# An attention-and-experts kernel whose build-time scheduler is switched to its detailed timing model

## The chip, the cores and the metric

The kernel runs on 1 core of one Trainium2 chip. The metric is the device time of one execution in microseconds (us); lower is better. The inputs come from a fixed seed.

## The reference, cut to what matters

Four batches of 10048 rows of width 128 pass through an attention with 49 agents, and the resulting 40192 rows through a mixture of 16 experts (4 groups of 4), of which each row takes one.

```python
def _attn_ref(q, k, v, agents):
    def sm(a, b):                      # softmax of scale * a b^T
        ...
    a2k = sm(agents, k)
    agent_v = a2k @ v
    q2a = sm(q, agents)
    return (q2a @ agent_v)
def _moe_ref(x, w_group, w_expert, w1, w2):
    ...                                # best group, then best expert of that group
            h = np.maximum(xg[mask_e] @ w1[g, e], 0.0)
            ye = h @ w2[g, e]
            out[tok_idx] = combined[:, None] * ye
```

## The kernel before

**Stages.** The work goes through the batches in the order `SEQ = (1, 2, 3, 0)`. An opening (to about 54 us) does keys, values and agents of the first batch and chooses the expert that most of its rows take. Then come three batches of *own tiles*: 20 tiles of 512 rows each, and each tile is sent through the batch's main expert in 8 *units*, 480 units in all. The last batch is *sorted*: its rows are scattered by expert into `sorted_rows` and read back in order, 164 units more, from about 720 us on.

**A unit** (functions `first`, `evicted`, `second`) is: on TensorE (PE) two matmuls of 512 columns into a PSUM bank `ph`, from the turned weights `et` of the tile and the expert's `wbuf`; on ScalarE (ACT) `hh<-ph`, the relu in 16 bits; on VectorE (DVE) `hl<-ph,hh`, what the 16 bits left over; then on PE three matmuls into `po`, two from `hh` and one from `hl`. `ph` has three banks (pool `ps1`), so the `ph` pair of a unit has to wait for the `hl` of the third unit before. In the source `second` runs `LAG = 8` units behind `first`.

```python
LAG = 8
            pending.append(first(x, k))
            for _ in range(2):
                if len(pending) > LAG:
                    run_second()
            advance(at + (k + 1) * each)
```

**Side work.** Beside the units of one batch runs the attention of the next. `advance` steps *lanes* (generators) after each unit and gives out so much ACT and DVE work per unit (`RATE`, 900 and 1100 ns); a lane that yields `HOP` rests for 2 units, so that what the next step reads is there. The names in it: `xf` are loaded keys or queries, `xh` (ACT) and `xl` (GpSimd, POOL) their 16-bit halves, and PE's `at<-agh,xl` the scores; `S` holds the scores of the keys, 10 tiles to a chunk, 8 chunks. `key_max` sends the maxima through PE (`at<-dg,ones`) and back to `mb` on DVE. `value_less` then subtracts it on DVE (`S<-S,mb`), `value_exp` takes the exponent on ACT (`S<-S,shift`), `value_split` makes `sh` and `vh` (ACT), `vl` (DVE) and `sl` (POOL), and `value_products` are PE's `at<-sh,vh`. The source steps these stages chunk by chunk (`skewed`). `mq`, `ef` and `rows` are the same for queries, `es` and the turned `et` come from them; `oo<-po,oo` on DVE ends a tile, with factors that were loaded from `cwt`.

**What sets the order.** The source gives each engine a program order; on leaving the `TileContext` at line 1847 a scheduler goes through all instructions and writes the order in which each engine gets them, which is fixed from then on. Each engine works its list off strictly in order: an instruction that waits holds up all behind it. Nearly all instructions are recorded by one helper and so stand at line 140.

## Time and profile before

| | |
|---|---|
| median of 3 runs | 914.24 us (911.54 to 914.42) |
| the profiled execution, its own time | 907.38 us |
| its span | 905.1 us |
| PE busy | 844.7 us, 93% |
| DVE busy | 710.8 us, 79% |
| ACT busy | 613.8 us, 68% |
| POOL busy | 462.9 us, 51% |
| mean granted TensorE clock | 0.982 of full speed |

Busy is the time in which an engine worked at any instruction; PE's matmuls overlap, so their single durations are longer than the distance at which they follow each other. The difference of 2.3 us between time and span lies ahead of the first and behind the last instruction. The profiled execution is 6.9 us shorter than the median of the three runs.

### The profile page before, as it was taken

Reading aid. Unit: us, or ns where it says so; the run is one execution under the profiler, and the core shown is the slowest. Engines: PE = TensorE matmul, PEld = TensorE weight load, DVE = VectorE, ACT = ScalarE, POOL = GpSimd, SP = SyncE. Lnnn points to the kernel's source line nnn. Section 1 sums busy time; section 2 is a strip of 40 time slices with the busy share of each in tenths; the row PEclk is TensorE's granted clock in tenths of the full one; section 3 lists DMA queues with packets and bytes.
Section 4 is the critical chain, followed back from the end, with each engine's and each line's share of the span. In section 5 each row is a group of like instructions: output and inputs, shape, how many; then the busy total and the mean of one; then the engine's idle time right before and its main releaser. Section 6 shows DMA issues by size and latency. Waiting matters only on the chain.

```text
span 905.1 us, 22546 instructions
## 1 busy us (share of the span) xinstructions
PE 844.7 (93%) x8668; PEld 502.2 (55%) x8669; DVE 710.8 (79%) x1442; ACT 613.8 (68%) x1078; POOL 462.9 (51%) x616
## 2 busy tenths in 40 slices
PE   4889999999797999898999999999999999999995
PEld 3745455555354555454455555554444477777775
DVE  7767898886799886688989689799977666766663
ACT  6568897867486777677678787766565555555552
POOL 4387495446426451838474343646555214444454
PEclk9989999999899999999999999999999999999998
DMA  9677436453554564434536222334756445555542
GB/s 360 245 244 272 139 108 225 157 163 128 173 170 130 169 196 147 156 115 152 169 112 242 83 75 104 112 102 151 230 176 212 138 140 165 174 190 187 176 141 98
DMA packets 58578, 149.95 MB, mean 166 GB/s; under 512 B 8702, under 2 KB 19830, under 8 KB 58460
## 3 DMA queue, kind: packets, MB, share of 16 engines
q1 hardware_dynamic: 53307, 138.11, 45.4%
q0 software_dynamic: 5152, 10.30, 3.2%
q8 instruction: 70, 1.15, 0.5%
q14 instruction: 49, 0.39, 0.1%
HBM read 108.33 MB, written 38.71 MB: 162 GB/s over the span
## 4 chain that ended last, share of the span: by engine, by line
PE 41%; DVE 8%; ACT 3%; DMA 2%; issue 2%; POOL 2%; POOLq 0%; ACTq 0%; DVEq 0%
PE po L140 24%; PE ph L140 12%; PE at L140 6%; DVE hl L140 3%; POOL xl L304 1%; ACT hh L140 1%; DMA out<-oo,er 1%; DVE vl L140 1%; DMA vf<-v 1%; DVE mq L140 1%; DVE ef L140 1%; ACT vh L140 1%; DVE oo L140 0%; POOL out L1485 0%; ACT es L140 0%
## 5 line engine op out<-in xcount | busy, mean ns | idle before, releaser
L140 DVE SCALAR_TENSOR_TENSOR hl<-ph,hh 128x512 f16<-128x512 f32 (+1 forms) x562 | 374.6, 677 | 125.7 <-ACT hh L140 122.0
L140 ACT ACTIVATE hh<-ph 128x512 f16<-128x512 f32 (+1 forms) x562 | 330.0, 594 | 188.2 <-PE ph L140 110.5
L140 PEld LDWEIGHTS <-wbuf 128*128 128x128 f16 (+2 forms) x2812 | 241.2, 97 | 282.6 <-issue 50.3
L140 PE MATMUL ph<-et,wbuf 98*128 98x512 f16 (+2 forms) x1048 | 317.4, 378 | 17.7 <-DVE hl L140 17.1
L140 PE MATMUL po<-hh,wbuf 128*128 128x512 f16 (+1 forms) x960 | 287.2, 379 | 0.0
L304 POOL TENSOR_TENSOR xl<-xf,xh 128x256 f16<-128x256 f32 x278 | 183.2, 696 | 137.1 <-ACT xh L140 124.4
L140 PE MATMUL po<-hl,wbuf 128*128 128x512 f16 (+1 forms) x480 | 181.3, 378 | 0.0
L1485 POOL DMA_INDIRECT out<-oo,er x82 | 80.7, 984 | 110.7 <-ACT hh L140 53.0
L140 PE MATMUL po<-wbuf,hh 128*128 128x128 f16 x1312 | 116.6, 219 | 0.0
L1199 POOL DMA_INDIRECT sorted_rows<-rows,slot x79 | 79.0, 1000 | 67.7 <-ACT hh L140 47.1
L140 PE MATMUL po<-wbuf,hl 128*128 128x128 f16 x656 | 112.9, 219 | 0.0
L140 PEld LDWEIGHTS <-hh 128*128 128x128 f16 x1312 | 99.2, 98 | 9.0 <-issue 9.0
L140 ACT ACTIVATE xh<-xf 128x1280 f16<-128x1280 f32 (+2 forms) x58 | 72.5, 1255 | 17.2 <-PE at L140 12.2
L510 POOL TENSOR_TENSOR sl<-S,sh 128x245 f16<-128x245 f32 (+2 forms) x51 | 37.8, 764 | 53.5 <-ACT sh L140 53.5
L140 PEld LDWEIGHTS <-hl 128*128 128x128 f16 x656 | 64.2, 98 | 0.0
L847 POOL TENSOR_TENSOR rows<-ef,rows 128x245 f16<-128x245 f32 (+1 forms) x62 | 39.9, 666 | 42.8 <-ACT rows L140 42.8
L140 PEld LDWEIGHTS <-xh 128*128 128x128 f16 x1166 | 46.3, 98 | 21.6 <-issue 2.2
L140 DVE SCALAR_TENSOR_TENSOR hl<-at,hh 128x512 f16<-128x512 f32 x82 | 55.8, 680 | 0.0
L140 DVE SCALAR_TENSOR_TENSOR vl<-vf,vh 128x640 f16<-128x640 f32 (+2 forms) x51 | 48.4, 956 | 7.2 <-ACT vh L140 7.2
L140 ACT ACTIVATE et<-at 98x512 f16<-98x512 f16 (+3 forms) x81 | 47.4, 596 | 8.8 <-PE at L140 8.7
L140 ACT ACTIVATE hh<-at 128x512 f16<-128x512 f32 x82 | 49.5, 604 | 0.0
L140 DVE TENSOR_TENSOR oo<-po,oo 128x512 f32<-128x512 f32 (+1 forms) x60 | 40.3, 672 | 9.6 <-PE po L140 6.2
(330 smaller groups left out, 1042.8 us busy)
## 6 DMA issues: line engine op xcount, KB each, us to landing
wbuf<-wdr SPq DMA_DIRECT2D x22, 832.0 KB
vf<-v SPq DMA_DIRECT2D x28, 645.0 KB
xf<-qT SPq DMA_DIRECT2D x27, 640.0 KB
xf<-kT SPq DMA_DIRECT2D x25, 640.0 KB
cols<-oo SPq DMA_DIRECT2D x60, 256.0 KB
oo<-cwt SPq DMA_DIRECT2D x57, 256.0 KB
erow<-rows SPq DMA_DIRECT2D x12, 490.0 KB
er<-sorted_rows SPq DMA_DIRECT2D x19, 256.0 KB
```

The costliest lines, as they stand in the source:

```text
L140: ins = f(*a, **k)
L304: pool.tensor_sub(out=xl[:, a:z], in0=xf[:, a:z], in1=xh[:, a:z])
L510: pool.tensor_sub(out=sl[0:m, y][:, z], in0=x[:, z], in1=sh[0:m, y][:, z])
L847: pool.tensor_sub(out=x0[:, a:z, NA:2 * NA], in0=ef[:, a:z], in1=x0[:, a:z, 0:NA])
L1199: ins = pool.indirect_dma_start(out=sorted_rows[:, :], out_offset=bass.IndirectOffsetOnAxis(ap=at, axis=0), in_=x, in_offset=None, bounds_ ...
L1485: ins = pool.indirect_dma_start(out=out, out_offset=bass.IndirectOffsetOnAxis(ap=to, axis=0), in_=y, in_offset=None, bounds_check=N - 1, o ...
```

## The change

The `TileContext` is told to schedule with its detailed timing model. No line of the computation is touched, no instruction is added or taken away: the same 8,552 matmuls, 1,441 DVE, 1,076 ACT and 611 POOL instructions and 422 loads and stores of the SP queue are put into another order.

```diff
-    with tile.TileContext(nc) as tc, ExitStack() as ctx:
+    with tile.TileContext(nc, schedule_with_timeline_sim=True) as tc, ExitStack() as ctx:
         build(ctx, tc, *args, out, cols)
```

What moves: of PE's matmuls of the opening and the own tiles hardly one keeps its place (by as much as 169 places), on DVE the places change by up to 58, on ACT by up to 32, on POOL by up to 20. In the sorted tiles, from about 720 us on, the order of all engines is the same as before but for a few neighbours. In the opening ACT takes the exponent `ef` of the first queries behind one `xh` more, and on SP one store to `sorted_rows` goes ahead of three loads. Three places show the pattern. In the names the number is that of the tile, so that the same name is the same buffer in both orders.

**DVE, the first batch's own units 33 to 45**, where the scores `S_834` of the next batch lose their maximum `mb_1827`. Before:

```order
L140 COPY mb_1827<-at_1800 128x49
L140 TENSOR_TENSOR S_834<-S_834,mb_1827 128x490
L140 SCALAR_TENSOR_TENSOR hl_1819<-ph_1815,hh_1818 128x512
L140 TENSOR_TENSOR oo_1718<-po_1720,oo_1718 128x512
L140 TENSOR_TENSOR S_834<-S_834,mb_1827 128x490
L140 SCALAR_TENSOR_TENSOR hl_1840<-ph_1836,hh_1839 128x512
L140 TENSOR_TENSOR S_834<-S_834,mb_1827 128x490
L140 SCALAR_TENSOR_TENSOR hl_1858<-ph_1854,hh_1857 128x512
L140 SCALAR_TENSOR_TENSOR vl_1852<-vf_1829,vh_1851 128x640
L140 SCALAR_TENSOR_TENSOR hl_1872<-ph_1868,hh_1871 128x512
L140 SCALAR_TENSOR_TENSOR hl_1884<-ph_1880,hh_1883 128x512
```

With the change:

```order
L140 COPY mb_1827<-at_1800 128x49
L140 SCALAR_TENSOR_TENSOR hl_1742<-ph_1738,hh_1741 128x512
L140 TENSOR_TENSOR S_834<-S_834,mb_1827 128x490 x3
L140 TENSOR_REDUCE mq_1956<-at_1774 128x10
L140 TENSOR_TENSOR S_834<-S_834,mb_1827 128x490 x4
L140 TENSOR_TENSOR S_834<-S_834,mb_1827 128x392
L140 TENSOR_TENSOR S_834<-S_834,mb_1827 64x49
L140 SCALAR_TENSOR_TENSOR hl_1753<-ph_1749,hh_1752 128x512
L140 SCALAR_TENSOR_TENSOR hl_1768<-ph_1764,hh_1767 128x512
```

The nine subtractions, which stood one or two between two `hl` over some 14 units, now stand in a row, with `mq` among them, ahead of `hl_1753`, the `hl` of unit 36. The same happens to the nine of the third batch (all nine between two `hl`) and of the fourth (eight of them and an `oo`).

**ACT, the same stretch**, where the exponents of these chunks are taken. Before:

```order
L140 ACTIVATE hh_1839<-ph_1836 128x512
L140 ACTIVATE S_834<-S_834,shift_122 128x490
L140 ACTIVATE vh_1851<-vf_1829 128x1280
L140 ACTIVATE hh_1857<-ph_1854 128x512
L140 ACTIVATE S_834<-S_834,shift_122 128x490
L140 ACTIVATE sh_1849<-S_834 128x490
L140 ACTIVATE hh_1871<-ph_1868 128x512
L140 ACTIVATE hh_1883<-ph_1880 128x512
L140 ACTIVATE S_834<-S_834,shift_122 128x490
L140 ACTIVATE hh_1913<-ph_1910 128x512
```

With the change:

```order
L140 ACTIVATE hh_1767<-ph_1764 128x512
L140 ACTIVATE S_834<-S_834,shift_122 128x490 x2
L140 ACTIVATE et_1925<-at_1920 98x512
L140 ACTIVATE sh_1849<-S_834 128x490
L140 ACTIVATE S_834<-S_834,shift_122 128x490
L140 ACTIVATE et_1932<-at_1927 98x512
L140 ACTIVATE sh_1988<-S_834 128x490
L140 ACTIVATE hh_1793<-ph_1790 128x512
L140 ACTIVATE S_834<-S_834,shift_122 128x490
L140 ACTIVATE et_1949<-at_1944 98x512
L140 ACTIVATE S_834<-S_834,shift_122 128x490 x3
L140 ACTIVATE S_834<-S_834,shift_122 128x392
L140 ACTIVATE S_834<-S_834,shift_122 64x49
```

Where one or two instructions stood between two `hh` in these rows, seven now stand between `hh_1767` and `hh_1793` and seven between `hh_1793` and `hh_1808` (the last row is followed by `hh_1808`).

**PE, unit 41 and the next**, the matmuls of `first` (into `ph`) and of `second` (from `hh` and `hl`). Before:

```order
L140 MATMUL ph_1836<-et_1677,wbuf0_90 128x512
L140 LDWEIGHTS wbuf0_90
L140 MATMUL ph_1836<-et_1677,wbuf0_90 128x512
L140 LDWEIGHTS wbuf0_90
L140 MATMUL po_1845<-hh_1714,wbuf0_90 128x512
L140 LDWEIGHTS wbuf0_90
L140 MATMUL po_1845<-hh_1714,wbuf0_90 128x512
L140 LDWEIGHTS wbuf0_90
L140 MATMUL po_1845<-hl_1715,wbuf0_90 128x512
L140 LDWEIGHTS wbuf0_90
L140 MATMUL ph_1854<-et_1677,wbuf0_90 128x512
```

With the change:

```order
L140 MATMUL ph_1836<-et_1677,wbuf0_90 128x512
L140 LDWEIGHTS wbuf0_90
L140 MATMUL ph_1836<-et_1677,wbuf0_90 128x512
L140 LDWEIGHTS wbuf0_90
L140 MATMUL po_1845<-hl_1794,wbuf0_90 128x512
L140 LDWEIGHTS wbuf0_90
L140 MATMUL po_1845<-hh_1808,wbuf0_90 128x512
L140 LDWEIGHTS wbuf0_90
L140 MATMUL po_1845<-hh_1808,wbuf0_90 128x512
L140 LDWEIGHTS wbuf0_90
L140 MATMUL ph_1854<-et_1677,wbuf0_90 128x512
```

Before, a `ph` pair is followed by the `po` matmuls of the unit eight earlier (`hh_1714` belongs to unit 33, `ph_1836` to unit 41). Now it is followed by the `hl` matmul of unit 38 (`hl_1794`) and the `hh` matmuls of unit 39 (`hh_1808`). In 406 of 449 units counted the `hl` matmul stands exactly three `ph` pairs behind its own, where it was eight.

## Rows read from the trace of the kernel before

**Rows 1.** The page: engines' busy time, share of span, instructions.
```profile
PE 844.7 (93%) x8668; PEld 502.2 (55%) x8669; DVE 710.8 (79%) x1442; ACT 613.8 (68%) x1078; POOL 462.9 (51%) x616
```

**Rows 2.** Busy time by stretch: start:end, length, PE, PEld, DVE, ACT, POOL, clock, DMA, GB/s.
```profile
0.00:75.00 75.00, 54.30 (x732) 39.22 (x734) 55.08 (x148) 49.33 (x77) 42.40 (x63) 0.93 0.78 288
75.00:640.00 565.00, 534.38 (x5094) 289.26 (x5092) 475.56 (x982) 420.90 (x733) 300.72 (x433) 0.98 0.44 147
600.00:720.00 120.00, 120.00 (x630) 56.16 (x629) 100.85 (x255) 73.03 (x127) 60.99 (x61) 1.00 0.54 177
720.00:890.00 170.00, 169.99 (x2338) 131.09 (x2336) 115.15 (x188) 94.22 (x185) 72.78 (x74) 1.00 0.50 167
```

**Rows 3.** Whom PE waited for from 75 to 640 us: total, times, longest.
```profile
PE ph L140 <- DVE hl L140: 16.7, 12, 5.6
PE at L140 <- POOL xl L304: 6.3, 7, 2.8
PE at L140 <- DVE vl L140: 1.5, 3, 0.6
PE at L140 <- ACT et L140: 1.4, 1, 1.4
PE at L140 <- DVE ef L140: 1.4, 2, 0.9
PE at L140 <- DVE cwo L140: 1.0, 2, 0.6
PE at L140 <- ACT es L140: 0.9, 2, 0.5
PE at L140 <- DVE dd L140: 0.7, 1, 0.7
```

**Rows 4.** Timeline of PE, units without side work: start, us, what.
```profile
104.94 0.60 PE L140 MATMUL ph<-et,wbuf 98*128 98x512 f16 x2
105.37 0.60 PE L140 MATMUL po<-hh,wbuf 128*128 128x512 f16 x2
105.80 0.38 PE L140 MATMUL po<-hl,wbuf 128*128 128x512 f16 x1
106.02 0.60 PE L140 MATMUL ph<-et,wbuf 98*128 98x512 f16 x2
```

**Rows 5.** Timeline of ACT and DVE, the same stretch.
```profile
105.57 0.60 ACT L140 ACTIVATE hh<-ph 128x512 f16<-128x512 f32 x1 [0.48 <-PE ph L140]
106.19 0.68 DVE L140 SCALAR_TENSOR_TENSOR hl<-ph,hh 128x512 f16<-128x512 f32 x1
...
108.81 0.66 DVE L140 TENSOR_TENSOR S<-S,mb 128x490 f32<-128x490 f32 x1
109.38 0.68 DVE L140 SCALAR_TENSOR_TENSOR hl<-ph,hh 128x512 f16<-128x512 f32 x1
...
109.97 0.69 ACT L140 ACTIVATE S<-S,shift 128x490 f32<-128x490 f32 x1
110.57 0.60 ACT L140 ACTIVATE sh<-S 128x490 f16<-128x490 f32 x1
111.07 1.07 ACT L140 ACTIVATE hh<-ph 128x512 f16<-128x512 f32 x2
```

**Rows 6.** Timeline of DVE, instructions that met POOL at work.
```profile
224.15 7.22 DVE L140 TENSOR_TENSOR coe<-coe,cog 128x16 f32<-128x16 f32 x1
284.91 3.57 DVE L140 SCALAR_TENSOR_TENSOR vl<-vf,vh 128x640 f16<-128x640 f32 x1
411.23 1.05 DVE L140 TENSOR_TENSOR S<-S,mb 128x490 f32<-128x490 f32 x1
```

**Rows 7.** Timeline of POOL and PE around two long waits.
```profile
218.73 12.61 POOL L304 TENSOR_TENSOR xl<-xf,xh 128x256 f16<-128x256 f32 x20
...
430.48 0.59 PE L140 MATMUL ph<-et,wbuf 98*128 98x512 f16 x2 [3.24 <-DVE hl L140]
```

**Rows 8.** Groups by form: count, busy us, mean ns, idle before.
```profile
L140 DVE TENSOR_TENSOR S<-S,mb 128x490 f32<-128x490 f32 x28 | 21.5, 792 | 0.1
L140 DVE TENSOR_REDUCE mq<-at 128x10 f32<-128x490 f32 x26 | 17.0, 656 | 3.5 <-PE at L140 3.4
L140 ACT ACTIVATE S<-S,shift 128x490 f32<-128x490 f32 x21 | 15.2, 723 | 1.0 <-DVE S L140 0.9
L140 ACT ACTIVATE xh<-xf 128x1280 f16<-128x1280 f32 x51 | 64.7, 1272 | 16.1 <-PE at L140 11.4 <-POOL xl L304 2.4 <-DVE vl L140 1.0
L304 POOL TENSOR_TENSOR xl<-xf,xh 128x256 f16<-128x256 f32 x271 | 181.0, 704 | 137.1 <-ACT xh L140 124.4 <-PE at L140 9.8 <-DMA vf<-v 2.5
```

**Rows 9.** Busy time and clock in the stretches of two waits, each with what followed.
```profile
226.40:231.40 5.00, 0.06 (x3) 0.00 (x0) 5.00 (x2) 1.27 (x1) 4.94 (x8) 0.95 0.16 52
231.40:237.40 6.00, 5.37 (x27) 2.31 (x27) 5.81 (x21) 1.76 (x4) 0.00 (x0) 0.50 0.34 89
380.70:384.50 3.80, 0.99 (x18) 0.50 (x15) 1.56 (x3) 1.45 (x2) 3.80 (x8) 1.00 0.70 229
384.60:387.80 3.20, 3.20 (x23) 1.55 (x22) 1.92 (x4) 2.24 (x5) 3.20 (x6) 0.50 0.69 210
```

## The prediction

> **What bounds the kernel now.** I read the engines' shares first: PE works in 93% of the span, the next engine in 79% [rows 1]. Then the stretches: from 600 us on PE never rests, and in the sorted tiles (720 to 890 us) it is busy all the time at full clock [rows 2]. So time can be won or lost in two places only: the opening, with some 21 us of PE idle in 75 us, and the own tiles from 75 to 640 us, where PE is busy for 534.4 of 565 us, which leaves 30.6 us idle [rows 2]. Whom PE waited for there [rows 3] gives 16.7 us to DVE's `hl`, 6.3 us to POOL's `xl` and 6.9 us to six smaller groups. The waits for `hl` are the third-unit rule: no bank, no next `ph`. The largest of them was no matter of order: one small DVE multiplication took 7.22 us [rows 6] while POOL went through 20 `xl` without a pause [rows 7]; another, 3.24 us, stands in [rows 7].
>
> The **slack of the bank loop** decides what an order may do. Without side work a unit takes PE 106.02 - 104.94 = 1.08 us, in it 0.43 us for `ph`, 0.43 for `po` from `hh`, 0.22 for `po` from `hl` [rows 4]. From the start of `ph` at 104.94 us to the end of its `hl` at 106.19 + 0.68 us [rows 5] it is 1.93 us. The bank is wanted after three units, 3.25 us. So ACT or DVE may fall behind by 1.3 us before PE stands; PE's own side work in those units makes it about 2.0 us at most places.
>
> **The change, part by part.** No work is added, so only idle time and clock can move.
>
> *Side work in rows on DVE and ACT: a loss.* At the first place of the printed order nine `S<-S,mb` and one `mq` stand between the `hl` of units 35 and 36. On DVE such a subtraction takes 0.57 us up to the next start (108.81 to 109.38 us) [rows 5], `mq` about the same less overlap [rows 8]. Seven full subtractions, a shorter one, the small one and `mq` make about 5.3 us, and `hl` ends 0.68 us later: 6.0 us behind the last `hl`. That one ends 1.93 us after the `ph` of unit 35 began, and the `ph` of unit 36 begins 0.93 us after it, by PE's matmuls in between; so the bank of unit 36 is free 1.0 + 6.0 = 7.0 us after its `ph` began. PE, by its own printed order with the prices of [rows 4], has 4.4 us of work until the `ph` of unit 39 asks for it. It stands for 2.6 us there. On ACT, exponents follow each other at 0.60 us (109.97 to 110.57 us) and others at 0.50 [rows 5]: seven between two `hh` are 3.7 to 4.1 us against 1.08 to 2.1 us of PE.
>
> I did the same addition for all units from the 12th to the 480th: what DVE (and ACT) has between two `hl` (two `hh`), at the mean of its form less the overlap, minus what PE has between the two `ph`; the excess is carried on, and what goes beyond the slack is PE's wait. The order before has at most 2.7 us of DVE work in one unit, none over 3.25; the new one has 12 units over 3.25 us on each of the two engines, up to 6.5. The sum over all units:
>
> - slack 1.3 us: 5.8 us before, 47.5 us now
> - slack 1.6 us: 3.8 before, 38.6 now
> - slack 2.0 us: 1.8 before, 30.2 now
>
> I take 1.6, between the bare loop and the loaded one: **+35 us** (+28 to +42). Against the trace this method does well: PE's waits for `hl` were 16.7 us, of which the two with other causes (7.2 us on DVE made the longest wait, 5.6 us, and 3.24 us) leave 7.9.
>
> *PE's direct waits for side work: a gain.* Counted in the orders, 33 of 240 pieces of `xl` stood within three units of their `xh` before, some one unit behind it; now 10 of 235 do, and none nearer than three. `vl`, `vh` and `es`, which stood one unit ahead of their readers at worst, now stand two to three ahead. If all waits of PE but those for `hl` go, that is 6.3 + 1.5 + 1.4 + 1.4 + 1.0 + 0.9 + 0.7 = **-13 us** [rows 3]; if POOL's 0.70 us a piece [rows 8] makes them late as before, 0.
>
> *The second matmuls nearer to the first: nothing.* An `hl` matmul three units behind its `ph` comes just after a `ph` that needed the same `hl` done. So it waits for nothing new.
>
> *Clock: a loss.* Behind the wait at 226 us and behind that at 381 us the granted clock was 0.50, 1.2 GHz, for 6.0 and 3.2 us, after PE had done almost nothing for 5.0 us and 1.0 us of work in 3.8 us [rows 9]. A half-speed stretch of 3.2 us costs 1.6 us. The addition has six waits of 2.5 us or more where the trace has four; I take **+4 us** (0 to +8).
>
> *Opening, SP, POOL, sorted tiles.* In the opening the exponent that leads to the choice of the first expert goes behind one more `xh`, 1.27 us [rows 8], part of it under waits for loads: **+1 us** (-1 to +3). SP's loads keep, counted in the new order, four units or more between the release of their buffer and their first reader, over 4 us; POOL idles in half of the span [rows 1]: 0 for both, and 3.2 us more or less if a load such as that behind the 3.24 us [rows 7] is met or missed. Sorted tiles: same order, PE full [rows 2], 0.
>
> **Sum**: 35 - 13 + 4 + 1 = +27 us. On the profiled execution, 907.4 us, that is 934. The median of the runs shown stands 6.9 us above it, and the forecast is for the median: 914.2 + 27 = **941 us**.
>
> **Rivals.** *Faster: the rows lie in PE's shadow.* If PE is late at these places anyway, say because it stands at a side matmul that waits for the same `mb`, the nine subtractions run while nobody wants `hl`. Then the direct waits go (-13) and with them half-speed stretches (-5) and a third of the waits for `hl` (-5): 914 - 23 = 891 us. For it speaks that `mb` itself comes from PE and is waited for; against it that the `ph` of unit 36 is free to start in [rows 4]'s terms 0.93 us after that of unit 35. It decides from a slack of 3.2 us on, where the addition falls to the 13 us that are won. Chance 0.15.
>
> *Slower still: DVE and POOL get in each other's way.* A subtraction took 0.66 us at 108.8 us [rows 5], 1.05 us at 411 us [rows 6], and 0.79 us as a mean [rows 8], and the two longest DVE instructions are of the same sort [rows 6]. If all 27 subtractions of the three rows meet POOL at work, 27 x 0.4 = 11 us come on top, all of it at places where PE already stands: 952 us. The Trainium skill, SBUF — State Buffer, section "Who interferes with whom", says that a VectorE instruction with two SBUF inputs contends with a GpSimd instruction that reads SBUF, and that whoever comes second is blocked for the whole of the other's instruction. The trace agrees in kind (7.22 us [rows 6]), though the mean of 0.79 us says that most do not meet. Chance 0.20.
>
> *No change.* The addition overstates: rows cost 13 us, direct waits give 13 back. 914 us. Chance 0.07.
>
> **Numbers.** Forecast 0.58, with its own range of 922 to 965 us from the ends of the terms. A run of this kernel can tell about 0.3% (3 us) from no change. Faster by more: 0.15; same: 0.07; slower: 0.58 + 0.20 = 0.78. The range from 905 to 970 us takes in the forecast, the two nearer rivals and a part of the faster one, and leaves out some 0.11 below and 0.07 above.
>
> **What would show it.** Right: from 75 to 640 us (some 25 us longer) PE's waits for `hl` grow from 16.7 to some 50 us, with 2.5 to 4 us each near the three rows of nine `S<-S,mb`; its waits for `xl` fall below 2 us; the clock of that stretch falls from 0.98; the time from the first sorted unit to the end is the same to 1 us. Wrong: waits for `hl` stay below 25 us, which says the loop has more slack than 2 us; or the loss is in the opening or in the sorted tiles, which says that I looked at the wrong place; or DVE waits long for PE inside the rows, which is the first rival.

## The result and the profile after

The changed kernel takes 923.38 us, median of 4 runs (919.85 to 925.72), against 914.33 (911.54 to 914.64) for the kernel before in the same comparison. The ratio is 1.0114, 95% interval 1.0089 to 1.0139: slower by 1.1%, some 9 to 10 us. The forecast was 27 us. The profiled execution took 919.85 us, its span is 918.1 us, its mean granted clock 0.980 (before: 907.38, 905.1 and 0.982).

The page of the changed kernel, busy time of the engines, answering to [rows 1]:

```profile
PE 853.3 (93%) x8668; PEld 504.1 (55%) x8669; DVE 707.0 (77%) x1442; ACT 615.3 (67%) x1078; POOL 459.1 (50%) x616
```

No work was added (the counts are the same), yet PE is busy for 8.6 us longer. The stretches of the changed kernel, with the columns of [rows 2]:

```profile
0.00:75.00 75.00, 49.08 (x698) 36.99 (x700) 51.12 (x142) 45.03 (x69) 40.14 (x57) 0.89 0.73 277
75.00:640.00 565.00, 538.73 (x5177) 293.54 (x5174) 474.77 (x1003) 422.90 (x738) 296.31 (x436) 0.99 0.47 154
...
720.00:890.00 170.00, 167.76 (x2154) 121.97 (x2151) 108.63 (x176) 91.19 (x175) 67.64 (x69) 1.00 0.46 154
```

Three things are to be seen. In the opening PE is busy for 5.2 us less than before. In the own tiles, where the forecast put all of its loss, it is idle for 565 - 538.73 = 26.3 us, less than the 30.6 us of before. And in the sorted tiles PE is busy nearly all the time, but gets through 2154 matmuls in 170 us where it got through 2338 [rows 2].

Whom PE waited for from 75 to 640 us, in the changed kernel, answering to [rows 3]:

```profile
PE ph L140 <- DVE hl L140: 16.6, 18, 4.8
PE at L140 <- ACT et L140: 2.2, 2, 1.4
PE at L140 <- DMA w1f<-w: 1.9, 1, 1.9
PE po L140 <- ACT hh L140: 1.9, 3, 1.1
PE at L140 <- DVE vl L140: 1.0, 3, 0.6
...
PE at L140 <- POOL xl L304: 0.2, 1, 0.2
```

The waits for `hl` are 16.6 us, as before, and not the 50 of the forecast. Those for `xl` are gone, as forecast.

Matching the same instruction in both traces gives the place of the loss. The table has the start of the `ph` pair of a unit, the time before and by how much the changed kernel is later. Units 1 to 480 are the own tiles; from 481 on only those units of the sorted tiles are counted that have a bank `ph`, which are 82 of 164:

| unit | 1 | 35 | 45 | 120 | 130 | 280 | 483 | 514 | 538 | 562 |
|---|---|---|---|---|---|---|---|---|---|---|
| before, us | 53.9 | 98.7 | 111.6 | 220.8 | 243.1 | 470.7 | 729.9 | 791.6 | 840.6 | 889.6 |
| later by, us | 5.1 | 9.4 | 18.3 | 13.5 | 5.4 | -3.5 | -0.1 | 4.2 | 7.6 | 11.7 |

The change loses 18 us by unit 45, gets all of it back by unit 483 (8 us of it between units 120 and 130, where the kernel before waits behind the `coe` of 7.22 us [rows 6] and then runs at half clock [rows 9]), and then loses 12 us at an even rate in the sorted tiles, where I had forecast none.

**The sorted tiles.** There a group of four units (`first_group`, lines 1392 to 1408) does four 512-column matmuls with `et` and then four with `rest`, the last 19 rows of the products, which lie in four strips of partitions, a strip for each unit. Timeline of PE before, the end of one group:

```profile
763.27 0.38 PE L140 MATMUL at<-et,wbuf 128*128 128x512 f16 x1
763.58 0.39 PE L140 MATMUL ph<-rest,wbuf 19*128 19x512 f16 x1
763.59 0.38 PE L140 MATMUL at<-rest,wbuf 19*128 19x512 f16 x1
763.59 0.39 PE L140 MATMUL ph<-rest,wbuf 19*128 19x512 f16 x1
763.59 0.38 PE L140 MATMUL at<-rest,wbuf 19*128 19x512 f16 x1
763.91 0.29 PE L140 MATMUL po<-wbuf,hh 128*128 128x128 f16 x2
```

The four strip matmuls start within 0.01 us and together take as long as one of them alone: 0.33 us to the next `po`, where the single strip of the next timeline takes 0.32. Timeline of PE in the changed kernel, the same group:

```profile
756.25 0.38 PE L140 MATMUL ph<-et,wbuf 128*128 128x512 f16 x1
756.56 0.39 PE L140 MATMUL ph<-rest,wbuf 19*128 19x512 f16 x1
756.88 0.39 PE L140 MATMUL at<-et,wbuf 128*128 128x512 f16 x1
757.20 0.38 PE L140 MATMUL at<-rest,wbuf 19*128 19x512 f16 x1
757.20 0.39 PE L140 MATMUL ph<-rest,wbuf 19*128 19x512 f16 x1
757.21 0.38 PE L140 MATMUL at<-rest,wbuf 19*128 19x512 f16 x1
757.52 0.29 PE L140 MATMUL po<-wbuf,hh 128*128 128x128 f16 x2
```

One strip has moved ahead of the fourth `et` matmul by a single place, and the others no longer start beside it: they start 0.64 us later. The 176 strip matmuls begin in 64 such stretches, against 41 before.

**The opening.** Timeline of PE around the scores of the first queries (`at<-agh,xh`, `at<-agh,xl`), first before, then the changed kernel:

```profile
36.96 0.20 PE L140 MATMUL at<-agl,xh 128*128 128x49 f16 x1
37.00 0.28 PE L140 MATMUL at<-agh,xl 128*128 128x49 f16 x5
37.21 2.54 PE L140 MATMUL at<-vf,S 128*49 128x129 f32 x38
```

```profile
37.28 0.18 PE L140 MATMUL at<-agl,xh 128*128 128x49 f16 x1
37.39 3.64 PE L140 MATMUL at<-vf,S 128*49 128x129 f32 x58
40.97 0.30 PE L140 MATMUL at<-agh,xl 128*128 128x49 f16 x5
```

The second half of the query scores now stands behind 58 products of values, 3.6 us. `mq`, which waits for the scores, starts 4.4 us later, and `ef`, `usum` and the choice of the first expert follow it; that is most of the 5.1 us by which unit 1 is late. `mq` on DVE before, then in the changed kernel:

```profile
37.32 0.67 DVE L140 TENSOR_REDUCE mq<-at 128x10 f32<-128x490 f32 x1 [1.06 <-PE at L140]
```

```profile
41.68 0.67 DVE L140 TENSOR_REDUCE mq<-at 128x10 f32<-128x490 f32 x1 [1.64 <-PE at L140]
```

**The row of subtractions.** At the first place of the forecast, DVE and then PE of the changed kernel, and the clock behind the wait:

```profile
111.32 1.82 DVE L140 TENSOR_TENSOR S<-S,mb 128x490 f32<-128x490 f32 x3
113.05 0.66 DVE L140 TENSOR_REDUCE mq<-at 128x10 f32<-128x490 f32 x1
113.63 4.73 DVE L140 TENSOR_TENSOR S<-S,mb 128x490 f32<-128x490 f32 x6
118.29 1.27 DVE L140 SCALAR_TENSOR_TENSOR hl<-ph,hh 128x512 f16<-128x512 f32 x2
```

```profile
113.84 0.38 PE L140 MATMUL at<-ident,rows 128*98 128x128 f16 x4
119.02 1.01 PE L140 MATMUL ph<-et,wbuf 98*128 98x512 f16 x2 [4.79 <-DVE hl L140]
```

```profile
116.30:123.10 6.80, 4.08 (x10) 1.47 (x10) 5.36 (x9) 5.64 (x12) 6.80 (x11) 0.50 0.00 0
```

This wait came where it was computed, and was longer: 4.8 us (the forecast had 2.6 us for DVE's row, and 2.5 to 4 us near each of the three rows), then 6.8 us at a granted clock of 0.50, 1.2 GHz, after PE had stood. But the nine subtractions near unit 136 have only waits of 0.8 and 1.1 us beside them, for `et` and `hh`. Those near unit 235 have two:

```profile
401.57 0.33 PE L140 MATMUL at<-ident,rows 128*98 128x128 f16 x3 [1.42 <-ACT et L140]
403.58 1.01 PE L140 MATMUL ph<-et,wbuf 98*128 98x512 f16 x2 [1.69 <-DVE hl L140]
```

Behind them PE runs at half clock for another 6.8 us. The three rows together have 9.8 us of waits.

### The profile page after: what moved, and what is told of

It is laid out like the page before. It is cut to its first block, busy times and chain, and to the rows that moved or that the text cites. A ratio compares the mean times of both kernels' runs of the same rounds, so it can differ in the third digit from the quotient of the medians.

```text
span 918.1 us, 22538 instructions
## 1 busy us (share of the span) xinstructions
PE 853.3 (93%) x8668; PEld 504.1 (55%) x8669; DVE 707.0 (77%) x1442; ACT 615.3 (67%) x1078; POOL 459.1 (50%) x616
## 4 chain that ended last, share of the span: by engine, by line
PE 67%; DVE 15%; ACT 6%; DMA 5%; issue 4%; POOL 2%; SPq 1%; POOLq 0%; ACTq 0%; DVEq 0%
PE po L140 34%; PE ph L140 20%; PE at L140 13%; DVE hl L140 5%; ACT hh L140 2%; DMA xf<-kT 2%; ACT xh L140 2%; DVE S L140 1%; DVE vl L140 1%; ACT S L140 1%; POOL out L1485 1%; DMA oo<-cwt 1%; DVE oo L140 1%; POOL xl L304 1%; DMA cwt<-cwc 1%
## 5 line engine op out<-in xcount | busy, mean ns | idle before, releaser
L140 ACT ACTIVATE hh<-ph 128x512 f16<-128x512 f32 (+1 forms) x562 | 325.3, 592 | 215.1 <-PE ph L140 135.5
L140 PEld LDWEIGHTS <-wbuf 128*128 128x128 f16 (+2 forms) x2812 | 235.0, 97 | 270.5 <-issue 63.0
L304 POOL TENSOR_TENSOR xl<-xf,xh 128x256 f16<-128x256 f32 x278 | 188.0, 711 | 139.1 <-ACT xh L140 126.8
L140 PEld LDWEIGHTS <-xh 128*128 128x128 f16 x1166 | 52.1, 97 | 27.9 <-ACT xh L140 0.8
L510 POOL TENSOR_TENSOR sl<-S,sh 128x245 f16<-128x245 f32 (+2 forms) x51 | 33.7, 684 | 61.2 <-ACT sh L140 61.2
L847 POOL TENSOR_TENSOR rows<-ef,rows 128x245 f16<-128x245 f32 (+1 forms) x62 | 37.9, 633 | 42.4 <-ACT rows L140 39.4
L140 PE MATMUL at<-agl,xh 128*128 128x49 f16 (+1 forms) x543 | 51.1, 184 | 0.0
L140 PE MATMUL at<-agh,xh 128*128 128x49 f16 (+1 forms) x543 | 50.3, 185 | 0.1
```

The costliest lines, as they stand in the source:

```text
L140: ins = f(*a, **k)
L304: pool.tensor_sub(out=xl[:, a:z], in0=xf[:, a:z], in1=xh[:, a:z])
L510: pool.tensor_sub(out=sl[0:m, y][:, z], in0=x[:, z], in1=sh[0:m, y][:, z])
L847: pool.tensor_sub(out=x0[:, a:z, NA:2 * NA], in0=ef[:, a:z], in1=x0[:, a:z, 0:NA])
```

## The experiments

Times vary from run to run (the kernel with the strips together from 905.6 to 916.6 us), so each ratio is to runs of the kernel before on the same chip, with its 95% interval; it is not the quotient of the two medians, from which it differs by up to 0.2 points. An edit is either a pin (`tc.keep_in_program_order`, which keeps an instruction behind what is written ahead of it on its engine, with no wait) or a chain of such edges through a list of instructions in a given order.

| kernel | ratio | interval |
|---|---|---|
| the change | 1.0114 | 1.0089 to 1.0139 |
| e1 change, strips kept together | 0.9992 | 0.9964 to 1.0020 |
| e2 before, strips split | 1.0166 | 1.0137 to 1.0194 |
| e3 change, opening pinned | 1.0222 | 1.0192 to 1.0252 |
| e4 change, rows taken apart | 1.0104 | 1.0077 to 1.0132 |
| e5 before, opening of the change | 1.0072 | 1.0056 to 1.0087 |
| e6 before, DVE and ACT of the change | 1.0710 | 1.0665 to 1.0755 |
| e7 e1 and the old opening | 1.0015 | 0.9997 to 1.0033 |
| e8 e7 and rows taken apart | 1.0036 | 1.0022 to 1.0050 |
| e9 before, a pause on POOL | 0.9936 | 0.9916 to 0.9956 |
| e10 e1, old order to unit 115 | 0.9799 | 0.9786 to 0.9812 |
| e11 e1, DVE and ACT in the old order | 1.0105 | 1.0084 to 1.0125 |
| e12 change, PE in the old order | 1.0392 | 1.0373 to 1.0411 |
| e13 e7, a pause on POOL | 0.9896 | 0.9874 to 0.9918 |
| e14 e8, a pause on POOL | 0.9916 | 0.9886 to 0.9946 |
| e15 e1, old order to unit 60 | 0.9825 | 0.9802 to 0.9849 |

### The split strips: e1 and e2

```diff
-                pe.matmul(ps[:, j * m:(j + 1) * m], x["wb"][s, f:f + P], x["rest"][s, 0:m], start=False, stop=(j == per - 1))
+                tc.keep_in_program_order(pe.matmul(ps[:, j * m:(j + 1) * m], x["wb"][s, f:f + P], x["rest"][s, 0:m], start=False, stop=(j == per - 1)))
```

> The changed kernel with one pin more: in first_group each of the four strip matmuls (ph/at <- rest, 19 rows each on row groups of their own) stays behind the instruction written ahead of it on PE, so that no 512-column matmul with et comes in between. The 176 strip matmuls then begin in 42 stretches, where the changed kernel has 64 and the kernel before 41. Theory 'split strips': a stretch takes 317 to 327 ns whether it holds one strip matmul or four, so 22 stretches less give 22 x 0.317 = 7.0 us back, all of it behind 720 us: about 916.4 us against 923.4. Rival 'the sorted tiles lose to something else' (pauses that the profile calls issue, transfers, the drain): less than 2 us back, 921 to 924. Rival 'rows of side work', on which the recorded sum rests: 0, since nothing moves ahead of 720 us.

911.81 us, ratio 0.9992. Against the change's 1.0114 that is 1.22 points, 11 us. In its trace (of its slowest run, 916.55 us) unit 483 is 8.0 us later than before and unit 562 8.3: in the sorted tiles 0.3 us are lost in place of 11.8. e2 turns it round, in the kernel before (all `et` matmuls are pinned, and the strips too):

```diff
+            if per == 1 and i == GROUP - 1:
+                tc.keep_in_program_order(strip(x, 0, *parts[0], per, m))
             for j in range(per):
                 f = (k * per + j) * P
-                pe.matmul(ps[:, j * m:(j + 1) * m], x["wb"][:, f:f + P], x["et"][:, 0:m], start=(j == 0), stop=False)
+                tc.keep_in_program_order(pe.matmul(ps[:, j * m:(j + 1) * m], x["wb"][:, f:f + P], x["et"][:, 0:m], start=(j == 0), stop=False))
```

> The kernel before, its scheduler untouched, with the split written by hand: in each group of four whole units the first strip matmul goes ahead of the fourth matmul with et, and PE keeps that order. 79 stretches of strip matmuls in place of 41. Theory 'split strips': 38 x 0.317 = +12.0 us, about 926.4 us against 914.3, all behind 720 us. Rivals: if strips cost the same apart as together, or the stage is bound by its evictions, within 2 us of the kernel before.

927.64 us, 1.66% or 15 us, where 12 were expected. Both runs moved by more than expected because a split was priced at 0.317 us. Start-to-start distances in the traces tell what it costs: `et` to `et` 216 ns, `et` to a strip 312, a strip to `et` 317 and, behind a strip that stood alone, `et` to the next strip 321, the strips to what follows 317. A whole group takes 3 x 216 + 312 + 317 = 1277 ns; a split one 2 x 216 + 312 + 317 + 321 + 317 = 1699. That is 0.42 us a split: 16 us for the 38 of e2, 9.3 for the 22 of e1. The 11 us that e1 gave are known to some 3 us only, but the traces have nearly the same: 11.8 us lost in the sorted tiles against 0.3. The 2.2 us over 9.3 stand in the trace of the changed kernel as seven pauses of PE from 720 to 890 us (170 - 167.76), up to 0.45 us each, that the profile puts down to issue but for 0.2 us. e3 and e4, which split the same strips, have 2.1 us of pauses each between their first strip and their last, e1 0.2 and the kernel before none; but e2, with 38 splits, has a single one, of 1.4 us. Why they come was not tried.

### The opening: e3, e5, e7

```diff
-        act.activation(xh[:, 0:n], xf[:, 0:n], AF.Copy)
+        placed(act.activation(xh[:, 0:n], xf[:, 0:n], AF.Copy))
...
-            vec.tensor_sub(out=xl[:, 0:a], in0=xf[:, 0:a], in1=xh[:, 0:a])
+            placed(vec.tensor_sub(out=xl[:, 0:a], in0=xf[:, 0:a], in1=xh[:, 0:a]))
```

(`placed` pins, in the opening only.)

> The changed kernel with the conversions of the opening (xh and xs on ACT, xl and xs on DVE, of the early chunks) pinned behind what is written ahead of them, so that they no longer pass the scores' copies, mx, odd and ef. Theory 'the opening lost 5 us': the first weights are fetched 3 to 5 us earlier and unit 1 begins at 54 to 56 us in place of 59.1; the end follows, 918.4 to 920.4 us. Rival 'the time is taken up by a later wait': unit 1 earlier but the end within 1 us of 923.4. Against the theory too: if the order of DVE's S and most rows, which this moves as well, holds up mx by as much as the conversions did.

931.73 us, 1.1 points slower than the change itself. The pin was the wrong edit: it also held back the `xh` that the first query scores need, from 19.8 us to 39.9, and `mq` came at 46.8 us. It shows how much hangs on this chain, not what the change lost. So the next runs took the order of PE, DVE and ACT in the opening from one kernel into the other:

```diff
+    placed = {i.name: i for i in nc.cur_bb.bb.instructions}
+    for line in OPENING_ORDER:
+        kept = [f"I-{n}" for n in line if f"I-{n}" in placed]
+        for a, b in zip(kept, kept[1:]):
+            tc.add_manual_dep(placed[b], a, mybir.DependencyInfo(mybir.DependencyClass.NoSync, mybir.DependencyReason.DATA), reason="order of the opening")
```

> The kernel before, its scheduler untouched, with one thing of the change alone: the 42 instructions of ACT, 87 of DVE and 417 of PE that are written ahead of the first unit keep the order that the changed kernel has for them. Theory 'the opening lost 5 us': the conversions pass mx, odd and ef, the first weights are fetched 5 us later, unit 1 begins at 59 us in place of 53.9, and nothing behind gives it back: +5 us, ratio 1.004 to 1.007. Rival 'given back later': unit 1 later but the end within 1 us. The recorded sum gave the opening +1 us.

915.43 us, +0.72%, 6.5 us. Unit 1 is 6.0 us later than before, and unit 562 8.0: the loss is real, six times the forecast term, and in this kernel nothing gives it back. The edit moves the whole order of the opening; that it is the 58 products which cost most of this is read from the timelines and was not tried by itself.

> The changed kernel with the strips kept together and the opening of PE, ACT and DVE in the order of the kernel before. If strips and opening are the two losses, it stands where the own tiles' order alone puts it: the strips gave 11 us, the opening gives 5 more: about 6 us under the kernel before, ratio 0.992 to 0.996. If the opening is given back later, it equals the run with the strips alone, ratio 0.999.

910.11 us, ratio 1.0015: no gain over e1. Unit 1 came at 55.5 us in place of 58.9, but at unit 13 there is a new wait of 6.7 us. Timelines of DVE, POOL and PE, and the stretch behind it, in e7:

```profile
72.80 7.70 DVE L140 SCALAR_TENSOR_TENSOR rs<-rs,ozz 128x8 f32<-128x8 f32 x1
```

```profile
71.01 9.47 POOL L311 TENSOR_TENSOR xl<-xf,xh 128x256 f16<-128x256 f32 x15
```

```profile
81.15 1.01 PE L140 MATMUL ph<-et,wbuf 98*128 98x512 f16 x2 [6.74 <-DVE hl L140]
```

```profile
79.20:86.00 6.80, 4.85 (x12) 1.76 (x12) 5.24 (x10) 1.19 (x2) 1.28 (x3) 0.50 0.01 2
```

A DVE instruction of 8 columns took 7.7 us, until POOL came to the end of its row (71.01 + 9.47 us). It is the sort of [rows 6] and [rows 7]; such an instruction is called held from here on.

### An instruction held by POOL: e9 and e13

e9 leaves all the orders of PE, DVE and POOL in the kernel before and adds one wait, so that POOL's row of 20 has a pause:

```diff
+    placed = {i.name: i for i in nc.cur_bb.bb.instructions}
+    for n in range(4023, 4028):
+        tc.add_manual_dep(placed[f"I-{n}"], "I-3914", mybir.DependencyInfo(mybir.DependencyClass.Sync, mybir.DependencyReason.DATA), reason="a pause in POOL's row")
```

> The kernel before with all orders kept and one wait more: on POOL the row of 20 pieces of xl pauses ahead of its sixteenth piece until DVE's coe<-coe,cog is done. In the kernel before that operation of 16 columns takes 7.22 us, to the end of POOL's row; in the changed kernel, where the row has pauses, 0.18 us. Theory 'held by a row of POOL without a pause': coe takes under 1.2 us, PE's wait of 5.6 us behind it goes, the end comes 4 to 6 us earlier, ratio 0.993 to 0.996. If the wait only moves to xl, which POOL now ends up to 1 us later, or to the hl behind, ratio 0.998 to 1.001.

904.12 us, ratio 0.9936, 5.8 us less. DVE and POOL in e9:

```profile
226.05 1.37 DVE L140 TENSOR_TENSOR coe<-coe,cog 128x16 f32<-128x16 f32 x1
```

```profile
221.04 6.35 POOL L304 TENSOR_TENSOR xl<-xf,xh 128x256 f16<-128x256 f32 x10
227.65 6.33 POOL L304 TENSOR_TENSOR xl<-xf,xh 128x256 f16<-128x256 f32 x10 [0.26 <-ACT hh L140]
```

A pause of 0.26 us between two pieces was enough: 7.22 us became 1.37. (It came ahead of the eleventh piece of the row and not, as expected, of the sixteenth.) `coe` ended at 227.42 us, 0.03 us behind the last piece ahead of the pause. e13 does the same to e7, with POOL's sixth piece behind `rs<-rs,ozz` and `rs<-rs`:

> The kernel with the strips kept together and the old opening (ratio 1.0015), all orders kept, with one wait more: POOL's row of 15 pieces of xl pauses ahead of its sixth until DVE's two operations rs<-rs,ozz and rs<-rs are done. There rs<-rs,ozz, 8 columns, took 7.70 us, to the end of the row, PE waited 6.7 us at unit 13, and a stretch of 6.8 us at half clock followed. Theory 'the old opening's 5 us are there but a held operation takes their place': rs under 2 us, the wait and the half clock go, 7 to 10 us less, ratio 0.990 to 0.994. Rival 'the opening is given back for want of conversions done ahead': the wait at unit 13 stays for xl or xh, ratio 0.999 to 1.003.

901.70 us, ratio 0.9896: 1.2 points under e7, 0.96 under e1. So the opening's loss is there in the changed kernel as well; what the old one gave in e7 was hidden by a held instruction.

### The rows of side work: e4, e8, e14

```diff
-            vec.tensor_sub(out=x, in0=x, in1=mb[0:m].broadcast_to([m, y.stop - y.start, NA]))
+            tc.keep_in_program_order(vec.tensor_sub(out=x, in0=x, in1=mb[0:m].broadcast_to([m, y.stop - y.start, NA])))
...
-            act.activation(x, x, AF.Exp, bias=shift[0:m])
+            tc.keep_in_program_order(act.activation(x, x, AF.Exp, bias=shift[0:m]))
```

> The changed kernel with the subtractions S<-S,mb and the exponentials of the later batches' agents pinned behind what is written ahead of them; the nine in a row at units 36, 136 and 235 are now one or two at a time, 10 to 20 instructions apart. The recorded theory (rows of side work, carried over units): its sum at a slack of 1.6 us falls from 38.6 to 22.6, so 16 us less, about 907 us. Theory 'PE is not ahead there, only the first row costs': the 5.0 us wait at unit 39 goes and with it the stretch at half clock behind it (6.8 us at half clock, 3.4 us), the other two rows give 0 to 3: 5 to 10 us, 913 to 918 us. If a half-clock stretch comes elsewhere instead, 5 us only. Rival 'no effect': the wait moves to the exponentials' other neighbours, 922 to 924 us.

922.01 us, ratio 1.0104 against 1.0114: no difference that can be told, and both theories missed. In the trace (of its fastest run, 915.82 us) the wait at unit 39 is gone (unit 45 is 9.9 us later than before, in place of 18.3), but by unit 100 it is 13.4 against 15.6. PE's idle time from 75 to 640 us is 565 - 540.48 = 24.5 us against 26.3; of its waits for `hl`, 16.3 us in 23 pieces are left, where there were 16.6 in 18:

```profile
75.00:640.00 565.00, 540.48 (x5175) 293.97 (x5173) 479.83 (x1012) 422.57 (x741) 300.16 (x438) 1.00 0.47 154
```

```profile
PE ph L140 <- DVE hl L140: 16.3, 23, 2.0
```

> The same with the subtractions and exponentials of the later agents pinned as well, so that their rows are taken apart. The recorded theory: the carried sum falls from 39.2 to 22.8, 16 us less than without the pin. Theory 'rows cost nothing but the wait at unit 39, which other waits replace': within 3 us of the run without the pin, as in the pin's run on the changed kernel (1.3 us, inside its interval).

912.39 us, ratio 1.0036: with the old opening the pin gains nothing either (0.2 points more than e7, inside the intervals). `rs<-rs,ozz` was held there as well, for 7.44 us.

> The same pause in the kernel that also has the rows of the later agents taken apart (ratio 1.0036, rs<-rs,ozz 7.44 us there, 10.2 us at half clock behind). Theory of the held operation: 7 to 11 us less, ratio 0.992 to 0.996. If the row at units 35 to 45 costs 5 us and half a stretch, it is now 4 to 8 us under the run before it, ratio 0.983 to 0.988; if other waits replace that one, as they did in the changed kernel, within 3 us of it.

904.27 us, ratio 0.9916 against 0.9896 for e13, inside the intervals. With the held instruction out of the way too, taking the rows apart gives nothing.

### Crossing the orders: e6, e11, e12

All three chain the instructions behind the opening, as above.

> The kernel before, its own opening, with DVE and ACT behind the opening in the order of the changed kernel, rows of side work and all; PE and POOL are ordered by the old scheduler around them, and 44 stretches of strips are there in place of 41 (3 x 0.42 = 1.3 us). The recorded theory (rows of side work, carried): the sum at a slack of 1.6 us is 51.4 us against 3.8, so +35 to +48 us, 945 us and more. Theory 'PE's idle time is a matter of the whole load and not of rows': within 6 us of the kernel before either way, ratio 0.994 to 1.007, with the waits of PE in the units behind the opening between 25 and 36 us in all, as in both kernels.

975.40 us, ratio 1.071: the second theory is far off, and the recorded one has the right sign and too small a size (66 us, where it had 35 to 48). One DVE instruction, `rs<-rs,ozz`, was held for 4.35 us here. PE, ordered by the old scheduler, is idle for 565 - 507.54 = 57.5 us, against 26.3 with nearly the same order of DVE and ACT in the changed kernel:

```profile
75.00:640.00 565.00, 507.54 (x4748) 270.35 (x4746) 416.63 (x827) 379.03 (x665) 260.09 (x398) 0.97 0.42 135
```

```profile
PE ph L140 <- DVE hl L140: 31.4, 34, 4.7
PE at L140 <- DVE vl L140: 5.5, 13, 1.3
PE at L140 <- POOL xl L310: 5.2, 5, 2.2
```

> The changed kernel with the strips kept together and DVE and ACT behind the opening in the order of the kernel before; PE and POOL are ordered around them on the detailed model. The recorded theory: the carried sum is 14.6 us in place of 38.6, so 24 us under the run with the strips alone, ratio 0.973. Theory 'the sum does not order the kernels; what counts is that PE's order is made for that of DVE and ACT by the same scheduler': ratio 0.99 to 1.01. If any crossing of one scheduler's DVE and ACT with the other's PE is as bad as the side work of after under the old scheduler (+7.1%): 1.03 to 1.07.

917.88 us, ratio 1.0105: just outside what the second theory allowed, 3.7 points from the recorded one. Without the rows it is 1.1 points slower than e1, which has them. `coe<-coe,cog` was held for 4.59 us there and a `vl` for 3.56. Where the 1.1 points lie is not shown: from 75 to 640 us PE is idle for 565 - 538.85 = 26.2 us, no more than in the changed kernel.

> The changed kernel with PE behind the opening in the order of the kernel before (41 stretches of strips with it); DVE and ACT are ordered around it on the detailed model. The recorded theory: the carried sum is 25.0 us, 13.6 less than 38.6, and the strips give 11: ratio 0.985. Theory 'PE's order must fit': with PE's side matmuls fixed, DVE and ACT are placed to suit, ratio 0.99 to 1.01, PE's waits of the own tiles 25 to 35 us in all. If crossing is bad in itself: 1.03 to 1.07.

944.46 us, ratio 1.0392, as crossing would have it. Waits for `hl` are 39.1 us, the longest 7.1; three DVE instructions were held for 8.5, 5.4 and 3.9 us, so POOL has a part in it that these runs don't separate. All three crossed runs lose: e6 7.1 points against the kernel before, e11 1.1 against e1, e12 2.8 against the change, though its strips are not split. That orders which one scheduler made for PE, DVE and ACT belong together is what this suggests; since each of the three also has held instructions, it is not shown apart from these.

### Where the new order is good: e10 and e15

> The changed kernel with the strips kept together, and what is written ahead of unit 115 in the order of the kernel before on PE, DVE, ACT and POOL. Up to unit 115 it should run as before (0 to +2 us), and behind it as the changed kernel. In the traces the changed kernel makes good 13.5 us between unit 120 and unit 483. Theory 'the new order is better behind unit 120': 5.6 us of coe and some 3 us of shorter waits remain, ratio 0.990 to 0.994. Rival 'it was only work done ahead': the new order has done 5 us more of PE's work by unit 140 and gets that back; the ratio is then 0.997 to 1.003.

890.41 us, ratio 0.9799: 18 us faster than the kernel before and the fastest of all, better than the theory had it. Here the two orders are not crossed but follow one another. The new order behind unit 115 with the strips together is worth 2%, and between units 115 and 483 the trace gains 15.6 us on the kernel before:

```profile
75.00:640.00 565.00, 547.57 (x5227) 298.06 (x5226) 483.01 (x1029) 430.12 (x753) 307.91 (x442) 1.00 0.48 157
```

```profile
PE ph L140 <- DVE hl L140: 7.7, 14, 1.7
PE at L140 <- ACT et L140: 2.9, 4, 1.4
PE at L140 <- DMA w1f<-w: 1.7, 1, 1.7
PE at L140 <- DVE vl L140: 1.4, 4, 0.6
```

PE is idle for 17.4 us of the 565, 13 less than before, its waits for `hl` are halved, none is longer than 1.7 us, and the clock rounds to 1.00 against 0.98 [rows 2] (3.4 us at half clock from 75 to 640 us, against 17.1 before). A part of this is `coe`, which took 1.53 us here: one pause on POOL gave 5.8 us in e9 with the old order.

> The changed kernel, strips together, with what is written ahead of unit 60 (not 115) in the order of the kernel before on PE, DVE, ACT and POOL. If all that the new order loses lies ahead of unit 60 (the traces have +17.8 us there against 13.5 at unit 120), it equals the run to unit 115: ratio 0.978 to 0.984. If units 60 to 115 hold part of it: 0.985 to 0.995.

895.23 us, ratio 0.9825. Most of what the new order loses lies ahead of unit 60; the 0.26 points up to unit 115 are within the two intervals.

## Why the prediction was right in sign by luck and wrong in size

The runs add up like this, in points of the kernel before: split strips +1.22 (the change to e1), the opening +0.96 (e1 to e13, with the pause), the rest of the order to unit 60 +0.71 (e13 to e15), units 60 to 115 +0.26 (e15 to e10), and the order behind unit 115 -2.01 (e10). Each step is the difference of two neighbouring kernels, so the sum is the measured +1.14 by construction; the first four are known to 0.3 to 0.4 points each, the last to 0.1. The forecast had a loss of 35 - 13 + 4 = 26 us in the own tiles, +1 in the opening and 0 in the sorted tiles. Measured, the own tiles give 0.71 + 0.26 - 2.01 = -1.04 points (e13, with its pause), some 9.5 us gained, and the whole loss is in the two places that were put at nothing or nearly so. That the sign came out right is luck.

**"Sorted tiles: same order, PE full, 0".** This step failed: 11 us were lost there (e1; 15 us in e2, with 38 splits for 22), more than the net result. I had seen that a few neighbours change places and took a busy PE for a PE at a constant rate. A matmul that comes into the midst of four that run side by side costs 0.42 us here, though PE is busy before and after. The first sign was in the timeline of the kernel before: four starts within 0.01 us. The Trainium skill, TensorEngine Tiling (Array Packing), section "Key Properties", says that tiles of the array operate independently and that changing the tiling mode drains the engine. The traces agree in kind: four strips in the time of one, and 312 to 321 ns at each change from or to a strip where `et` follows `et` at 216.

**"Opening: +1 us".** Failed: 6.5 us (e5). I followed one exponent on ACT behind one more `xh`, and did not follow what that exponent waits for; PE's own order had put 58 products ahead of the scores, and `mq` came 4.4 us later.

**"Side work in rows on DVE and ACT: +35 us".** This was the step that made the size wrong. The addition found the first row, where PE waits 4.8 us at unit 39, and the rows near 136 and 235 are met by waits too. Two things failed. The size: in place of 35 us the three rows have 9.8 us of waits, all waits for `hl` in the changed kernel are 16.6, and of the six waits of 2.5 us or more there is one. And how the sum was used: it was added to the idle time of before, 30.6 us less 13, as if the old waits for `hl` stayed. But of those 16.7 us [rows 3] 14.1 go with the old order, at units 124, 157 to 159, 255 and 256, the 5.6 us behind `coe` first of all (e9: 5.8 us for one pause). The text called that wait "no matter of order"; with the new order alone `coe` takes 0.18 us and the wait is gone. I had set it aside to claim that the addition "does well" (3.8 us computed where 7.9 were left over, which is half), and then left it in the sum. Nor does the sum rank kernels:

| kernel | sum at slack 1.6, us | PE idle 75 to 640, us |
|---|---|---|
| before | 3.8 | 30.6 |
| e11, old order of DVE and ACT | 14.6 | 26.2 |
| e4, rows apart | 22.6 | 24.5 |
| e12, old order of PE | 25.0 | 53.3 |
| the change | 38.6 | 26.3 |
| e6, same rows, PE by the old scheduler | 51.4 | 57.5 |

The sum leaves out direct waits and held instructions, and for the change it exceeds all of PE's idle time. That idle time is of about the same size in both orders, and taking rows apart (e4) hardly changes it. The text named this as what would show it wrong: waits for `hl` below 25 us, and the loss in the opening or in the sorted tiles. That the loop "has more slack than 2 us", as it went on, no run shows, and why the addition overstates the second and third row stays open.

**"Direct waits for side work: -13 us".** The mechanism was right for `xl`, 6.3 to 0.2 us; in all, direct waits fell from 13.2 to 9.0 us, since others came (`et`, `hh`, a load of `w1f`). A third of the term.

**"Clock: +4 us".** Not borne out: mean 0.980 against 0.982 in the profiled runs, and 0.99 against 0.98 from 75 to 640 us. Half-clock stretches of 6.8 us came behind the waits at units 39 and 238, 13.7 us in all, and the four behind the old waits, 17.1 us in all, went. Waits of 2.5 us or more are three in the trace of the kernel before from 75 to 640 us (5.6, 3.2 and 2.8), not the four of the text.

**The range.** "From the ends of the terms" the terms give 914 + 14 = 928 to 914 + 53 = 967 us, and not the 922 to 965 that stand there; the measured 923 lies below the first and just inside the second.

**The rivals.** The faster one, rows in PE's shadow, is partly right: the second row cost 1.9 us of waits, the third 3.1 and a half-clock stretch, and the direct waits fell by a third. Its 891 us is the time of e10, but there the first 115 units are the old ones, so this is no confirmation of it. The slower one named DVE and POOL, and priced it on the subtractions: their mean went from 792 ns [rows 8] to 765, no loss. Its mechanism was the right thing to look at, in another place: small instructions held by a row on POOL.

## What to carry to other kernels

When a scheduler reorders a whole program, add up the waits of both orders by cause, take off all that the new order removes, and do not add a sum for the new order to the idle time of the old. Where PE is full, read the distances of its starts as well: 22 single exchanges of neighbours inside groups of matmuls that run side by side cost more here than all the other moves in the net. An order can be good in one stretch and bad in another: a hybrid (the old order to unit 115, then the new one, strips pinned) beat the kernel before by 2% and the changed one by 3%.

## What the runs showed of the hardware

- Four strip matmuls on row groups of their own start within 0.01 us and run in the time of one; an `et` matmul between them costs 0.42 us a group (1277 to 1699 ns; 15 us for 38 groups in e2).
- A DVE instruction of 8 or 16 columns with two inputs in SBUF was held for 7.0 to 7.7 us (`coe` before and in e2 and e5, `rs` in e7 and e8), over ten and more POOL instructions of 0.63 us each, and let go by the first pause, of 0.26 us in e9 and 0.93 in e13. It does not always happen: in the changed kernel `coe<-coe,cog` took 0.18 us while POOL was at work, and a `vl` took 1.45 us there and 5.29 in e1, at the same place of the order. The Trainium skill, SBUF — State Buffer, section "Who interferes with whom", has the blocked engine wait for the whole of the other's instruction; here the hold is longer than any one instruction.
